# A build-time dispatcher that orders all engines of an attention and token-MLP kernel, with the softmax denominators re-laid by DMA and the MLP and output projection in one PSUM bank

## Chip, core and metric

One core of a Trainium2 chip. The metric is device time in microseconds of one execution; three executions of the kernel before took 981.83, 982.70 and 983.78, so the median is 982.7.

## What is computed

Sequence length 2048, width 512, 32 heads of 16, MLP width 1376, all inputs bf16, and `B_x` is not used:

```python
xn = _layernorm(x)                       # the same normalised x feeds both branches
# A: full attention over 2048 keys, 32 heads of 16
qkv = xn @ wqkv
p = softmax(q @ k.T * 16 ** -0.5)        # per head, 2048 x 2048
a = (p @ v) @ wo
# B: an MLP over the tokens (w1: 2048 x 1376, w2: 1376 x 2048)
h = _layernorm(xn)
u = gelu(einsum("bsd,sf->bdf", h, w1) + b1)
y = einsum("bdf,fs->bds", u, w2) + b2
out = x + a + transpose(y)
```

There are 32 heads x 2048 x 2048 = 134 million exponentials, which is where the time goes.

## The kernel before

**Blocks, key tiles and units.** The attention runs in 32 blocks, `b = 8 * qb + G`: four query blocks of 512 rows (`qb`), and eight groups of four heads (`G = 2 * T + e_`). A block walks over 16 key tiles of 128 keys. For one key tile (the code calls it a period, or group `g`) TensorE makes four score matmuls, one per head, each on its own strip of 32 rows of the array (L748, `score_group`), into two *pairs* of PSUM banks. ScalarE takes the exponential of one pair at a time, 128 x 1024 elements (L757, `exp_pair`), into one of ten buffers `pT`. Four PV matmuls then add that key tile into bank 6 (L767, `pv_group`). V carries a 17th column of ones per head, so the same matmuls sum the denominators. Banks 0 to 5 are three pairs used in turn; in block 0 only two pairs are, since banks 4 and 5 serve the first tiles' transposes and V.

**Extras.** Everything else that TensorE does goes through one more bank, number 7 (`EX_BANK`): the Q, K and V projections of later blocks (L425, L407, L569), the 11 units of the first MLP matmul (`task_ut`, 16 matmuls each, L605, then three VectorE steps, a tanh on ScalarE at L620, and one VectorE step), the 16 units of the second (`task_yt`, 11 matmuls each, L632), and the output projection of 16 row tiles (`task_outproj`, 8 matmuls each, L652). VectorE must empty bank 7 before the next extra begins.

**Order of the work.** There is no scheduler on the chip: each engine runs its own list in order and waits on semaphores. The lists are written by one loop over periods. In each period it issues the scores and exps of one key tile, the PV of the tile two periods back, and then up to `EXTRA_BUDGET = 2.0` big matmuls from a queue of extras that is sorted by hand-written due periods. Due periods put the first MLP matmul after block 4, the second one right after it, and the output projection of query block `qb` near the end of the query block after it.

**End of a block.** Bank 6 is copied to `OT32` (L688). VectorE shuffles the four denominator rows over the partitions (L695) and inverts them in four pieces of 128 columns (L700). GpSimd multiplies (L703) and leaves `oT`, which the output projection reads. The last block uses a shorter way straight from bank 6 (L712 to L719), with the last two projection matmuls per tile and the stores interleaved.

**Residual.** `task_yt` writes `0.5 * y + x` plus the bias into an f32 buffer `resid`, which takes the place of `xn` and `h`; the output projection is added to it on the way out.

**Block 0.** After four tiles are prepared, block 0 starts, and the other twelve tiles' LayerNorm, transposes, K and V of T=0 are put one tile per period behind the PV matmuls.

Of the kernel before, what the change touches and what calls it, by code (L numbers as in the profile page):

```python
# [12 lines left out]
S = 2048  # L13
# [13 lines left out]
GELU_A = 0.044715  # L27

DEBUG_SCHED = False
LAG = 2  # L30
NPB = 10
NQS = 3
EXTRA_BUDGET = 2.0
NW1 = 2
NW2 = 2

# [148 lines left out]
def bass_parallel_sum__softmax_full_mha__mixer_token_mlp__prompt_kernel(  # L185
# [18 lines left out]
    with ExitStack() as es:  # L204
# [5 lines left out]
        x_sb = sb("x_sb", [128, NT, D], BF16)  # L210
# [3 lines left out]
        resid = big.bitcast(F32)[:, :].rearrange("p (t d) -> p t d", d=D)  # L214

        def resid_alias_keys(st):
            ks = []
            for j in (2 * st, 2 * st + 1):
                ks.append(("xn", j) if j < NT else ("h", j - NT))
            return ks  # L220
# [6 lines left out]
        V17 = sb("V17", [128, NKT * H * 17 + 16], BF16)  # L227
        pT = sb("pT", [128, NPB, 1024], BF16)
        OT32 = sb("OT32", [128, 2, 512], F32)
        denb = sb("denb", [128, 2, 512], F32)  # L230
# [12 lines left out]
        u_sb = sb("u_sb", [128, 1, 512], F32)  # L243
        ga_sb = sb("ga_sb", [128, 1, 512], F32)
        osb = sb("osb", [128, 2, 512], BF16)
        ps = es.enter_context(nc.psum_tensor("ps", [128, 8 * 512], F32))

# [8 lines left out]
        def bank_bf16(i):  # L256
            return ps.bitcast(BF16)[:, i * 1024:(i + 1) * 1024] if hasattr(ps, "bitcast") else None

# [3 lines left out]
        def dma(q, dst, src, reads, writes, name="", noncontig=False):  # L262
            if noncontig:
                def fn(eng, dst=dst, src=src):
                    with nc.allow_non_contiguous_dma(reason="tiny strided vector load"):
                        return eng.dma_start(dst, src)
            else:
                def fn(eng, dst=dst, src=src):
                    return eng.dma_start(dst, src)
            return sc.add(q, fn, reads=reads, writes=writes, name=name, dma=True)  # L270
# [8 lines left out]
        v17_kh = V17[:, 0:NKT * H * 17].rearrange("p (k h c) -> p k h c", k=NKT, c=17)  # L279
        for T in range(1, 4):  # L280
            sc.add("dve", lambda e, T=T: e.memset(v17_kh[:, :, 8 * T, 0:16], 0.0),
                   writes=[("V", t, T) for t in range(NT)])
        sc.add("dve", lambda e: e.memset(V17[:, NKT * H * 17:], 0.0), writes=[("Vpad",)])
        sc.add("dve", lambda e: e.memset(v17_main[:, :, 16:17], 1.0), writes=[("Vone",)])

        sc.add("pool", lambda e: e.memset(qmask[:, 0:1], 0.0), writes=[("qmask",)])
        for r in range(4):
            sc.add("pool", lambda e, r=r: e.memset(qmask[32 * r:32 * r + 16, 0:1], 1.0),
                   reads=[("qmask",)], writes=[("qmask",)])
        sc.add("pool", lambda e: e.tensor_scalar(qmask[:, 1:2], qmask[:, 0:1], -1.0, 1.0, ALU.mult, ALU.add),  # L290
# [69 lines left out]
        def ln_tile(t, which):  # L360
            ln_stats(t, which)
            ln_norm(t, which)
# [12 lines left out]

        ps_bf = ps.bitcast(BF16)

        def kt_chunk(T, c, bk, evac_eng="dve"):
            kt_pe(T, c, bk)
            kt_evac(T, c, bk, evac_eng)  # L380

        def kt_evac(T, c, bk, evac_eng):
            evac(evac_eng, KT[:, T, 512 * c:512 * (c + 1)], bank(bk), reads=[("bank", bk)],
                 writes=[("KTt", T, t) for t in range(4 * c, 4 * c + 4)])
# [14 lines left out]
        def kt_pe(T, c, bk):  # L399
            for _ in kt_pe_gen(T, c, bk):  # L400
                pass

        def kt_pe_gen(T, c, bk):
            for ct in range(NCT):
                if ct % 2 == 0:
                    yield 2.0
                sc.add("pe", lambda e, ct=ct: e.matmul(  # L407
                    bank(bk), lhsT=wqkv_sb[:, ct, D + 128 * T: D + 128 * T + 128],
                    rhs=xnT[:, ct, 512 * c:512 * (c + 1)], start=(ct == 0), stop=(ct == NCT - 1)),
                    reads=[("wqkv", 1, T)] + [("xnT", t) for t in range(4 * c, 4 * c + 4)], writes=[("bank", bk)])  # L410

        def evac(eng, dst, src, reads, writes):
            if eng == "act":
                return sc.add("act", lambda e: e.activation(dst, src, ACTF.Identity), reads=reads, writes=writes)
            return sc.add("dve", lambda e: e.tensor_copy(dst, src), reads=reads, writes=writes)  # L415

        def qt_proj(qb, T, bk, act_first=False):
            for _ in qt_proj_gen(qb, T, bk, act_first):
                pass

        def qt_proj_gen(qb, T, bk, act_first=False):
            for ct in range(NCT):
                if ct % 2 == 0:
                    yield 2.0
                sc.add("pe", lambda e, ct=ct: e.matmul(  # L425
                    bank(bk), lhsT=wqkv_sb[:, ct, 128 * T:128 * (T + 1)], rhs=xnT[:, ct, 512 * qb:512 * (qb + 1)],
                    start=(ct == 0), stop=(ct == NCT - 1)),
                    reads=[("wqkv", 0, T)] + [("xnT", t) for t in range(4 * qb, 4 * qb + 4)], writes=[("bank", bk)])
            yield 0.0
            for e_ in range(2):  # L430
                b = 8 * qb + 2 * T + e_
                slot = b % NQS
                if act_first and e_ == 0:
                    sc.add("act", lambda e, slot=slot: e.activation(QT[:, slot, :], bank(bk), ACTF.Identity,
                                                                    scale=qmask[:, 0:1]),
                           reads=[("bank", bk), ("qmask",)], writes=[("QT", slot)])
                else:
                    sc.add("dve", lambda e, e_=e_, slot=slot: e.tensor_scalar(QT[:, slot, :], bank(bk),  # L438
                                                                            qmask[:, e_:e_ + 1], None, ALU.mult),
                           reads=[("bank", bk), ("qmask",)], writes=[("QT", slot)])  # L440

        def vT_pe(tiles, T, bk):
            for j, t in enumerate(tiles):
                for ct in range(NCT):
                    sc.add("pe", lambda e, ct=ct, j=j, t=t: e.matmul(  # L445
                        bank(bk)[:, 128 * j:128 * (j + 1)], lhsT=xnT[:, ct, 128 * t:128 * (t + 1)],
                        rhs=wqkv_sb[:, ct, 2 * D + 128 * T:2 * D + 128 * (T + 1)],
                        start=(ct == 0), stop=(ct == NCT - 1)),
                        reads=[("wqkv", 2, T), ("xnT", t)], writes=[("bank", bk)])

        def vT_evac(tiles, T, bk, evac_eng):
            n = len(tiles)
            t0_ = tiles[0]
            assert tiles == list(range(t0_, t0_ + n))
            dst = V17[:, t0_ * H * 17:(t0_ + n) * H * 17].rearrange("p (t h c) -> p t h c", t=n, c=17)[:, :, 8 * T:8 * T + 8, 0:16]
# [3 lines left out]
        NPRE = 4  # L459
        SH = 0  # L460

        def tb(t):
            return t % 2 if t < NPRE else 4

# [514 lines left out]
```

## Time and profile before

| what | value |
|---|---|
| median of three runs | 982.7 us |
| span of the profiled execution | 979.6 us |
| ScalarE (ACT) busy | 953.8 us, 97% |
| TensorE (PE) busy, clock granted between 1.0 and 0.5 | 822.8 us, 84% |
| VectorE (DVE) busy | 306.4 us, 31% |
| GpSimd (POOL) busy | 70.1 us, 7% |
| DMA | 18.34 MB, mean 19 GB/s |

The profiled execution has no device time of its own in the results; its span runs from the first to the last instruction of the program, and the median of the runs is 3.1 us longer. PEld is the load of the stationary operand, and SPq the DMA queue of SyncE. A line of the timeline is: start, duration, engine, source line, operation, output <- inputs, shape, count, and in brackets the idle time before it with what ended it; equal instructions are merged, so "x20" lasts from the first one's start to the last one's end. A line of the chain of waits is: start, duration, engine, output, source line, count. A line of the windows view is: the stretch, its length, then busy time (and count) of PE, PEld, DVE, ACT and POOL, the granted TensorE clock, the DMA share and GB/s.

### The profile page before, as it was taken

To read this page: it belongs to the slowest core of one execution; us is meant where nothing else is said; L and a number is where in the kernel's file an instruction comes from. 1 tells how busy PE (TensorE), PEld (TensorE's weight loads), DVE (VectorE), ACT (ScalarE), POOL (GpSimd) and SP (SyncE) were. 2 spreads that over 40 slices of the span, in tenths; PEclk is the share of its full clock that TensorE was granted. 3 is DMA by queue.
4 is the path that set the end of the run, shared out by engine and by line. 5 is a ranking of instruction groups with operands and counts; after the bars stand their busy time and mean duration, and the time that the engine had idled before them with its cause. 6 is when DMAs were issued, how large, how long until landed. Compare 5 with 4: busy or idle time off the path is not lost.

```text
span 979.6 us, 11965 instructions
## 1 busy us (share of the span) xinstructions
PE 822.8 (84%) x5019; PEld 208.2 (21%) x5084; DVE 306.4 (31%) x522; ACT 953.8 (97%) x1045; POOL 70.1 (7%) x110
## 2 busy tenths in 40 slices
PE   5888898787888878888888888989889898998885
PEld 3422213211111112222222222111211111111121
DVE  6666633234322343222333223122211212102233
ACT  5999999999999999999999999999999999999995
POOL 3213200000000000000000000000000000000000
PEclk9999859988878888999999999555955555555797
DMA  8000000122111100111011010000000000000000
GB/s 193 2 1 17 6 1 2 22 51 43 21 22 22 22 17 1 30 28 27 11 30 44 17 42 2 0 1 4 19 1 1 1 1 0 1 1 1 11 11 22
DMA packets 57013, 18.34 MB, mean 19 GB/s; under 512 B 50816, under 2 KB 56960, under 8 KB 56960
## 3 DMA queue, kind: packets, MB, share of 16 engines
q1 hardware_dynamic: 53792, 16.00, 7.1%
q10 hardware_dynamic: 3168, 1.57, 0.6%
q8 instruction: 40, 0.66, 0.3%
q14 instruction: 13, 0.11, 0.0%
HBM read 15.47 MB, written 2.10 MB: 18 GB/s over the span
## 4 chain that ended last, share of the span: by engine, by line
ACT 87%; PE 10%; DVE 2%; issue 1%; DMA 1%; ACTq 0%; SPq 0%; DVEq 0%
ACT pT L757 86%; PE ps L748 3%; PE ps L767 2%; PE ps L605 1%; PE ps L425 1%; DMA x_sb<-in_A_x_dram 1%; ACT ga_sb L620 1%; PE ps L389 0%; PE ps L407 0%; DVE denb L717 0%; PE ps L652 0%; DVE QT L438 0%; PE ps L445 0%; DVE osb L665 0%; DVE stats L341 0%
## 5 line engine op out<-in xcount | busy, mean ns | idle before, releaser
L757 ACT ACTIVATE pT<-ps 128x1024 bf16<-128x1024 f32 x1024 | 946.2, 1390 | 4.2 <-PE ps L748 2.6
L748 PE MATMUL ps<-QT,KT 32*128 32x512 bf16 x2048 | 448.9, 464 | 123.5 <-ACT pT L757 102.1
L767 PE MATMUL ps<-pT,V 128*32 128x512 bf16 x2048 | 240.3, 469 | 0.6 <-ACT pT L757 0.6
L748 PEld LDWEIGHTS ps<-QT,KT 32*128 32x128 bf16 x2048 | 95.3, 94 | 505.8 <-ACT pT L757 481.5
L688 DVE COPY OT<-ps 128x512 f32<-128x512 f32 x31 | 21.4, 692 | 322.0 <-PE ps L767 322.0
L700 DVE RECIPROCAL denb<-denb 128x128 f32<-128x128 f32 x124 | 108.8, 920 | 0.9
L703 POOL TENSOR_TENSOR oT<-OT,denb 128x512 bf16<-128x512 f32 x31 | 39.3, 1266 | 791.3 <-DVE denb L700 791.3
L767 PEld LDWEIGHTS ps<-pT,V 128*32 128x32 bf16 x2048 | 51.9, 97 | 148.1 <-issue 145.8
L605 PE MATMUL ps<-big,w1blk 128*128 128x512 bf16 (+1 forms) x158 | 54.5, 419 | 6.5 <-issue 3.6
L632 PE MATMUL ps<-gT,w2blk 128*128 128x512 bf16 (+1 forms) x160 | 53.0, 398 | 2.8 <-issue 1.8
L637 DVE SCALAR_TENSOR_TENSOR big<-ps,x_sb 128x512 f32<-128x512 f32 x16 | 11.1, 691 | 102.3 <-PE ps L632 102.3
L652 PE MATMUL ps<-wo_pad,oT 128*128 128x512 bf16 x107 | 35.5, 406 | 2.4 <-issue 1.7
L610 DVE TENSOR_SCALAR u_sb<-ps,b1col 128x512 f32<-128x512 f32 (+1 forms) x11 | 8.3, 751 | 74.3 <-PE ps L605 74.3
L438 DVE TENSOR_SCALAR QT<-ps,qmask 128x512 bf16<-128x512 f32 x30 | 21.1, 747 | 32.3 <-PE ps L425 32.3
L665 DVE TENSOR_TENSOR osb<-ps,big 128x512 bf16<-128x512 f32 x16 | 11.0, 688 | 52.1 <-PE ps L652 52.0
L425 PE MATMUL ps<-xnT,wqkv_sb 128*128 128x512 bf16 x49 | 21.4, 509 | 2.6 <-issue 2.6
L695 DVE STREAM_SHUFFLE denb<-OT 128x512 f32<-128x512 f32 x31 | 22.4, 721 | 0.0
L415 DVE CAST V<-ps 128x128 bf16<-128x128 f32 (+1 forms) x26 | 12.4, 477 | 22.8 <-PE ps L569 22.2
L347 POOL TENSOR_TENSOR mv<-mv,mhalf 128x1 f32<-128x1 f32 x32 | 18.2, 567 | 2.7
L407 PE MATMUL ps<-xnT,wqkv_sb 128*128 128x512 bf16 x42 | 14.7, 423 | 2.7 <-DVE KT L415 1.6
L605 PEld LDWEIGHTS ps<-big,w1blk 128*128 128x128 bf16 (+1 forms) x176 | 10.7, 101 | 28.4 <-issue 24.4
L415 DVE CAST KT<-ps 128x128 bf16<-128x128 f32 (+1 forms) x26 | 12.2, 469 | 14.4 <-PE ps L407 9.1
(59 smaller groups left out, 211.8 us busy)
## 6 DMA issues: line engine op xcount, KB each, us to landing
w1blk<-in_B_w_dram SPq DMA_DIRECT2D x10, 512.0 KB, 4.1
w2blk<-in_B_w_dram SPq DMA_DIRECT2D x16, 320.0 KB, 3.3
out_dram<-osb SPq DMA_DIRECT2D x16, 128.0 KB, 1.7
x_sb<-in_A_x_dram SPq DMA_DIRECT2D x3, 512.0 KB, 9.9
wqkv_sb<-in_A_wqkv_dram ACTq DMA_DIRECT2D x3, 384.0 KB, 11.2
wo_pad<-in_A_wo_dram SPq DMA_DIRECT2D x8, 64.0 KB, 2.0
wqkv_sb<-in_A_wqkv_dram ACTq DMA_DIRECT2D x3, 128.0 KB, 3.8
w2blk<-in_B_w_dram SPq DMA_DIRECT2D x16, 24.0 KB, 1.7
```

Of the source, the lines that this page charges most:

```text
L415: return sc.add("dve", lambda e: e.tensor_copy(dst, src), reads=reads, writes=writes)
L425: sc.add("pe", lambda e, ct=ct: e.matmul(bank(bk), lhsT=wqkv_sb[:, ct, 128 * T:128 * (T + 1)], rhs=xnT[:, ct, 512 * qb:512 * (qb + 1)], st ...
L605: sc.add("pe", lambda e, st=st: e.matmul(bank(EX_BANK)[0:m, :], lhsT=w1blk[:, slot, st, 0:m], rhs=h_sb[:, st, :], start=(st == 0), stop=(s ...
L632: sc.add("pe", lambda e, ft=ft, m=m: e.matmul(bank(EX_BANK), lhsT=w2blk[0:m, slot, ft, :], rhs=gT[0:m, ft, :], start=(ft == 0), stop=(ft = ...
L652: sc.add("pe", lambda e, G=G: e.matmul(bank(EX_BANK), lhsT=oT[:, par, G, 128 * sti:128 * (sti + 1)], rhs=wo_pad[:, G, :], start=(G == 0), ...
L688: sc.add("dve", lambda e: e.tensor_copy(OT32[:, eb, :], bank(PV_BANK)), reads=[("bank", PV_BANK)], writes=[("OT32", eb)])
L695: sc.add("dve", lambda e: e.stream_shuffle(denb[:, eb, :], OT32[:, eb, :], [16] * 32), reads=[("OT32", eb)], writes=[("denb", eb, c) for c ...
L700: sc.add("dve", lambda e, cs=cs: e.reciprocal(denb[:, eb, cs], denb[:, eb, cs]), reads=[("denb", eb, c)], writes=[("denb", eb, c)])
L703: sc.add("pool", lambda e: e.tensor_tensor(oT[:, qb % 2, G, :], OT32[:, eb, :], denb[:, eb, :], ALU.mult), reads=[("OT32", eb)] + [("denb" ...
L748: sc.add("pe", lambda e, r=r, bk=bk: e.matmul(bank(bk), lhsT=KT[32 * r:32 * r + 32, T, 128 * kt:128 * (kt + 1)], rhs=QT[32 * r:32 * r + 32 ...
L757: sc.add("act", lambda e: e.activation(pT[:, buf, :], ps[:, s_ * 1024:(s_ + 1) * 1024], ACTF.Exp, scale=0.25), reads=[("bank", 2 * s_), (" ...
L767: sc.add("pe", lambda e, r=r, buf=buf, off=off: e.matmul(bank(PV_BANK)[32 * r:32 * r + 32, :], lhsT=V17[:, off:off + 32], rhs=pT[:, buf, 5 ...
```

## The change

All the code that writes the engine lists is replaced. The instructions of a score pair, an exp, a PV round, a LayerNorm, a projection stay what they were unless listed here.

**A dispatcher at build time.** A small simulation with one table of estimated durations decides in which order instructions enter each engine's list. Every job is a generator that yields steps (engine, priority, ready test, action). Whenever an engine is free in the model, the ready step with the lowest priority value is issued and the engine is held for the estimated time:

```diff
+EST = dict(
+    start=15.5, pe_switch=0.11, mm512=0.215, mm128=0.065, pe_lat=0.25,
+    exp=0.924, exp_lat=1.45, tanh=0.75, act_lat=0.55,
...
+    pool_lat=0.1, rstd=0.95, pmul=1.3, sp=0.15, dma=2.3, dma_big=6.0,
+)
+class Dispatch:
...
+                    for ent in self.steps[e]:
+                        _, pr, ready, _ = ent[1]
+                        if not ready():
+                            continue
+                        pr = 0.9 if pr is None else pr
+                        k = (pr() if callable(pr) else pr, ent[0])
+                        if best is None or k < best[0]:
+                            best = (k, ent)
```

On PE a pair of scores has priority 0.0, a chunk of two extra matmuls 1.2 and PV a value that depends on how much is waiting; two key tiles' PV can be issued together:

```diff
+        def a_feed():
...
+                        def ready(b=b, kt=kt, T=T):
+                            return (any(is_free(("pair", i)) for i in range(3)) and done(("QT", b))
+                                    and k_ready(T, kt))
...
+                            for r in (2 * hf, 2 * hf + 1):
+                                score_mm(b, kt, r, 2 * s_ + r % 2)
...
+            if held >= NPB - 3 or len(c) >= 3:
+                return 0.8
+            if len(c) >= 2 or left_pv[b] <= 2:
+                return 1.4
+            return 5.0
...
+                per = 2 if cost is None else max(1, int(0.43 / cost))
```

Bank 7 goes to the extra with the earliest due period among those whose inputs are ready in the model, whether it is due yet or not. The queue has no budget per period any more:

```diff
+            for k, (due, rel, gen, nm) in enumerate(extras):
+                if (best is None or due < best[0]) and rel():
+                    best = (due, k)
```

**Exponentials.** The code also has a path that would make some exponentials on VectorE from bits (`d_score`, `d_bits`, `d_chain`, key tiles `D_KTS`). It is used for blocks `b >= D_FROM`, and `D_FROM = 99`, so with 32 blocks all 1024 exps stay on ScalarE. Q is scaled by `QSCALE` instead of 1 and the exp's scale divided by it. Four scalings of V into a new tile `VS` remain (`vs_scale`), and a memset of it on GpSimd in the prologue, ahead of the masks for Q.

**Denominators.** For all blocks but the last, the shuffle and the four reciprocals give way to DMAs, all on SP's queue, round one small reciprocal; GpSimd's multiply stays:

```diff
+                for r in range(4):
+                    dma("sp", rl[32 * r:32 * r + 32, eb, :],
+                        OT32[32 * r + 16:32 * r + 17, eb, :].rearrange("p (j c) -> p j c", c=16),
+                        reads=[("OT32", eb)], writes=[("rl", eb)], name="den_gather", noncontig=True)
...
+                sc.add("dve", lambda e: e.reciprocal(rl[:, eb, :], rl[:, eb, :]),
+                       reads=[("rl", eb)], writes=[("rl", eb)])
...
+                dma("sp", scr[eb].rearrange("r (j c) -> (r j) c", c=16), rl[:, eb, :],
+                    reads=[("rl", eb)], writes=[("scr", eb)], name="den_put", noncontig=True)
...
+                for r in range(4):
+                    dma("sp", denb[32 * r:32 * r + 32, :], scr[eb, r:r + 1, :].broadcast_to([32, 512]),
+                        reads=[("scr", eb)], writes=[("denb",)], name="den_spread")
```

`scr` is a small tensor in DRAM.

**Second MLP matmul and output projection in one bank.** `task_out(st)` replaces `task_yt` and `task_outproj`: 11 + 8 matmuls (11 + 6 in the last query block) add into bank 7, and one VectorE step adds bias and residual. The residual rows are read from DRAM a second time with the W2 blocks. The gelu's factor 0.5 moves into the step before it:

```diff
-                sc.add("pe", lambda e, ft=ft, m=m: e.matmul(
+                mms.append(lambda ft=ft, m=m: sc.add("pe", lambda e: e.matmul(
                     bank(EX_BANK), lhsT=w2blk[0:m, slot, ft, :], rhs=gT[0:m, ft, :],
...
+                    start=(ft == 0), stop=False),
+                    reads=[("w2blk", slot), ("gT", ft)], writes=[("bank", EX_BANK)]))
             for G in range(ng):
...
+                mms.append(lambda G=G: sc.add("pe", lambda e: e.matmul(
                     bank(EX_BANK), lhsT=oT[:, par, G, 128 * sti:128 * (sti + 1)], rhs=wo_pad[:, G, :],
...
+                    start=False, stop=(G == ng - 1)),
...
+                sc.add("dve", lambda e: e.scalar_tensor_tensor(dst, bank(EX_BANK), b2col[:, st:st + 1],
+                                                               xr[:, slot, :], ALU.add, ALU.add),
```

A tile's `task_out` may start when the first MLP matmul is complete, its W2 block is loaded, the tile before it is out, and `oT` of the query block's last group (of group 5 in the last query block) is there.

**Smaller edits.** `QT` has four slots instead of three, and one VectorE step writes both heads' versions of Q (`task_qt`). A W1 unit may start when the gelu of the one before is complete (`task_ut`). In block 0 a tile's transposes, K and V are separate jobs of the dispatcher (`tile_job`). The prologue's first four tiles and the last block's end keep their steps.

## The prediction

> **What bounds the kernel now.** First the page, for the engine that is always busy and for the clock.
>
> ```profile
> PE 822.8 (84%) x5019; PEld 208.2 (21%) x5084; DVE 306.4 (31%) x522; ACT 953.8 (97%) x1045; POOL 70.1 (7%) x110
> ACT  5999999999999999999999999999999999999995
> PEclk9999859988878888999999999555955555555797
> L757 ACT ACTIVATE pT<-ps 128x1024 bf16<-128x1024 f32 x1024 | 946.2, 1390 | 4.2 <-PE ps L748 2.6
> ```
>
> ScalarE is full from slice 2 to the last; its 1024 exps (L757) are the kernel, and they stay there. PE's 84% is not a bound, but its clock falls to half wherever only scores and PV are left (slices 29 on).
>
> ACT's share hides small losses, since an exp is issued before the one ahead has ended. So I take the pace from the longest unbroken piece of the chain of waits, 250.34 / 273 = 0.917 us.
>
> ```profile
> 394.52 250.34 ACT pT L757 x273
> 765.62 56.01 ACT pT L757 x61
> 824.40 56.01 ACT pT L757 x61
> ```
>
> By the timeline of ACT the first exp starts at 15.79 and the last ends at 968.14: 952.35 us. 1024 x 0.917 = 939.0, and 11 tanh at 0.52 (next fence) are 5.7. So **7.6 us** are lost between first and last exp, and no order of work can win more than that; the prologue (15.8) and the tail (11.5) keep their steps. Some 2 us of it lie in block 0 (ACT idles 0.98 at 22.52). The rest comes where extra matmuls meet a slow clock. The timeline round one W1 unit (first ACT, then PE):
>
> ```profile
> 204.42 0.81 ACT L620 ACTIVATE ga_sb<-ga_sb 128x512 f32<-128x512 f32 x1
> 204.94 18.96 ACT L757 ACTIVATE pT<-ps 128x1024 bf16<-128x1024 f32 x20
> 223.63 0.78 ACT L620 ACTIVATE ga_sb<-ga_sb 128x512 f32<-128x512 f32 x1
> 225.38 0.60 PE L748 MATMUL ps<-QT,KT 32*128 32x512 bf16 x2 [1.04 <-ACT pT L757]
> 225.92 0.62 PE L767 MATMUL ps<-pT,V 128*32 128x512 bf16 x4
> 226.47 1.03 PE L605 MATMUL ps<-big,w1blk 128*128 128x512 bf16 x2
> 227.44 0.61 PE L748 MATMUL ps<-QT,KT 32*128 32x512 bf16 x4
> ```
>
> A tanh costs 204.94 - 204.42 = 0.52. From tanh to tanh are 19.21 us: 20 exps and one tanh make 18.86, so 0.35 is lost per unit. On PE, start to start at half clock, a pair of scores takes 0.54 (225.38 to 225.92), a PV group 0.55, two big matmuls 0.97. The same at full clock:
>
> ```profile
> 213.88 0.39 PE L748 MATMUL ps<-QT,KT 32*128 32x512 bf16 x2 [0.26 <-ACT pT L757]
> 214.19 0.40 PE L767 MATMUL ps<-pT,V 128*32 128x512 bf16 x4
> 214.53 0.61 PE L605 MATMUL ps<-big,w1blk 128*128 128x512 bf16 x2
> 215.07 0.39 PE L748 MATMUL ps<-QT,KT 32*128 32x512 bf16 x2
> ```
>
> 0.31, 0.34, 0.54. Where the clock changes, from windows (the figure before the DMA share is the clock):
>
> ```profile
> 204.60:211.40 6.80, 5.47 (x27) 1.02 (x28) 2.39 (x4) 6.67 (x9) 1.27 (x1) 0.50 0.59 115
> 211.40:220.60 9.20, 8.02 (x57) 2.17 (x54) 0.00 (x0) 9.20 (x11) 0.00 (x0) 1.00 0.02 4
> 220.60:225.00 4.40, 2.57 (x19) 0.64 (x18) 2.69 (x4) 4.40 (x6) 0.00 (x0) 1.00 0.57 119
> 225.00:232.00 7.00, 6.28 (x31) 1.28 (x36) 3.40 (x7) 6.87 (x9) 0.00 (x0) 0.51 0.00 0
> ```
>
> The W1 burst ends at 220.6, 4.4 us without extras follow, the clock halves, and it stays half 5.4 us into the next burst (226.47 to 232).
>
> **The slack.** After the pair at 225.38 the next is due one pace later, 226.30; it comes at 227.44, 1.14 late. The one after (due 228.13) starts at 229.50, 1.37 late, and 0.35 is lost. A Q projection at half clock makes a pair 1.14 late (762.89 to 764.95 against 0.917), and there the cycle of two blocks takes 824.40 - 765.62 = 58.78, against 64 x 0.917 = 58.69: 0.1 lost. So scores may be about 1.0 us late; lateness beyond that is lost on ACT.
>
> **The change, part by part.**
>
> *The order.* Before, each key tile gets at most two big matmuls. The dispatcher gives scores priority, but whenever no pair of PSUM banks is free PE takes a chunk of two, as long as an extra holds the one extra bank: some chunk per exp. At full clock that fits (0.31 + 0.54 = 0.85 of 0.917, with PV deferred and doubled): 0 lost. Its cost table knows one clock only (0.215 per matmul, 0.11 per switch, the warm rows above). At half clock the modelled sequence pair, chunk, chunk, pair comes to 0.54 + 0.97 + 0.97 = 2.48, so the next pair is 1.56 late, and each further pair with chunk adds 1.51 - 0.92 = 0.59. Less 1.0 of slack: 0.5 for a burst of two chunks, 1.2 after the next pair.
>
> *W1 units.* A unit waits for the gelu of the one before: evacuation and two steps 0.75 + 0.69 + 0.69, tanh 0.78 with half a pace of waiting, 0.69, some 0.9 of latencies: 4.9 us, in which the clock falls as at 220.6. In the first four gaps K and V projections for T=3 run and keep it up; for six of eleven I count half clock. It reaches into the next burst for 2 to 5.4 us; the losses run from 0.4 to 1.8, I take **1.0 each, 6.0**.
>
> *MLP output and projection in one bank.* Now 19 matmuls per tile (17 in the last quarter), one evacuation instead of two, and the separate bias step goes: on VectorE about 16 x (0.69 + 0.49) = 19 us less, off the path (31% busy). But the W2 work, spread from 391 to 609 at full clock today, moves to four dense bursts after blocks 7, 15, 23 and 29, each after a stretch without extras. Same price: **4 x 1.0 = 4.0**. The last burst is 4 x 17 matmuls, some 38 us by a chunk per exp and 1.2 of evacuation, inside the 47 us or so that blocks 30 and 31 (58.7) leave after block 29's result, so it fits; if it didn't, the tail would grow by what is over, up to 10. Residual rows are read again, 16 x 128 KB beside the W2 loads: hidden, as a store of that size lands in 1.7 us.
>
> *Q projections.* Isolated at half clock: by the spans of blocks about eight (at b = 10, 14, 16, 18, 22, 24, 26, 30) instead of four. Two chunks back to back, bounds 0.1 (today's) and 0.8 (a PV behind them): **8 x 0.5 = 4.0**. One evacuation of 1024 columns for two of 0.747, between 0.75 and 1.5: hidden behind 16 periods of lead.
>
> *Block 0.* Only two bank pairs there; chunks of K, V and transposes now fall between any two scores instead of at one fixed place. Bounds 2.0 (today) and 7 (every one of 12 tiles late by 0.4): **3.5**, nearer today's since the matmuls are the same. The added memset of VS sits on POOL ahead of the LayerNorm steps: 17 times the columns of the 0.20 us one, at most 3.4, into gaps of 1.65 and 2.52; rows of x land only at 7.4: 0.
>
> *Denominators.* Out go 124 reciprocals (0.92) and 31 shuffles (0.72), 131 us of VectorE. In come 31 reciprocals of 16 columns (between 0 and 0.92) and 9 DMAs per block on SP's queue: gather, store to DRAM, spread. Each leg lands in about 1.7 to 2.0 (small loads and stores of before): copy, three legs, reciprocal, POOL's 1.27, about 8 to 9 us. Block 30's result has the whole of block 31 (29 us) as cover, block 31 keeps the old on-chip way; without cover 8 us would go on the end. What is queued behind the new waits: on VectorE the reciprocal waits for its gather, and the evacuation that frees the extra bank stands behind it, with PE's next extra and then scores behind that. Behind a 512 KB load (4.1 us) a gather is late by 2 or more; five such meetings, half of them felt. On POOL LayerNorm steps stand behind the multiply. Between 0 and 5: **1.0**.
>
> *Tanh.* The order on ACT is fixed from the model, with half a pace of margin on average; if PE ends a burst up to 1 us late, ACT waits: 0 to 5, **1.5**.
>
> Sum: 6.0 + 4.0 + 4.0 + 3.5 + 1.0 + 1.5 = 20.0 lost, against 7.6: +12.4. Span 979.6 + 12.4 = 992.0; the median of the three runs (982.7) lies 3.1 above the span, so **995.1**.
>
> The page "TensorE: Matmul & The Clock Gate" of the Trainium skill ("What's actually happening") says that one idle window of about 3.4 us halves the clock and one busy window restores it. That speaks against bursts with gaps; by its window a burst would run 3.4 us at half clock and lose about 0.9, ten of them 9 instead of 10; the rows above show up to 5.4.
>
> **Rivals.**
> 1. *Faster* (0.20): scores first keeps ACT fed, bursts warm the clock sooner and the slack takes nearly all. For it: W2 work at full clock lost nothing from 394 to 645. Block 0 at 2.0 and 1.5 for the rest: 4.1 less, 978.6. It decides where a pair at half clock stays under 1.0 late.
> 2. *Same* (0.06): the losses come to what they are today, 980.7 to 984.7.
> 3. *Denominator legs stall VectorE and PE* (0.10): gathers land 1.7 us later than planned in every block, less 1.0 of slack, 31 x 0.7 = 22 on top: 1017. Against it: all rows of small transfers.
> 4. That the change doesn't do what it says: the VectorE exponential path is never entered (D_FROM = 99); only four scalings of VS remain, under 1 us each, no price.
>
> The likeliest has 0.64, its own range 986 to 1010. With the faster rival and the edge of the third the range is **978 to 1012**. Faster by over 0.2% (2 us, what a measurement of this kernel can tell) 0.20, within 0.06, slower 0.74.
>
> **What would show it.** Right: exps at 0.917 wherever no extras run, the gaps between them longer at each W1 unit, after blocks 7, 15, 23 and 29 and at each lone Q projection, all at a clock of 0.5; L700's 124 rows gone. Wrong: W1 units at full clock throughout, losses under 8 in all, or VectorE idle in front of the small reciprocal for microseconds.

## The result, and the profile after

The changed kernel takes **1105.3 us** in the median of four runs (1092.4 to 1114.8), the kernel before 982.3 beside it: ratio **1.120**, interval 1.114 to 1.127. Executions more than 1.5% above the fastest of their kernel are left out of the ratios, and of the times given for `before_split` (there 1089.5 and 1090.9) and `legs_pace` (1119.7 and 1122.8, the one traced). The forecast was 995.1 with a range up to 1012. The profiled execution is the fastest of the four; its span is 1090.5, which is 110.9 more than before. The three others took 13 to 22 us longer, and no trace shows where.

From the page of the changed kernel, the lines that answer to those of before:

```profile
PE 984.7 (90%) x5033; PEld 221.6 (20%) x5084; DVE 165.6 (15%) x324; ACT 970.0 (89%) x1045; POOL 71.8 (7%) x111
ACT  5977967799797699999998979999999999999875
PEclk8966958578555585555555975555555985555685
L637 ACT ACTIVATE pT<-ps 128x1024 bf16<-128x1024 f32 x1024 | 960.6, 1267 | 95.8 <-PE ps L583 93.7
L767 DVE RECIPROCAL rl<-rl 128x16 f32<-128x16 f32 x31 | 7.8, 253 | 218.9 <-DMA rl<-OT 218.9
```

ScalarE's row of nines has holes in its first 14 slices (to 382 us), near 580 and 640 us and at the end, and its idle time before exps went from 4.2 to 95.8 us, nearly all of it waiting for scores (L583). PE's clock is at a half for most of the span although PE is 90% busy. VectorE, which lost half its work, sits 218.9 us in front of the small reciprocal (L767).

Counted as in the prediction (from one exp's end to the next, less 0.917, less 0.52 for each tanh between), before loses 7.5 us from the first exp's end to the last's and after 119.1; the difference, 111.6, is the whole of the 110.9. So everything is lost between exps, and the place of each loss can be read off. Block 0 to 58 us: 4.2. Six single gaps of 2.4 to 4.5 us, each behind a block's gathers: 19.7. One more of 1.65 at 88.5, behind a LayerNorm step of VectorE that took 3.61 us instead of 0.40 while GpSimd cleared `wo_pad` for 3.55. Eight lone Q projections at 0.66: 5.3. The remaining 88 come in bursts of extras, mostly in steps of 0.59 from one exp to the next.

**The single gaps.** The largest, in the chain of waits of the changed kernel (start, length, engine, output, line):

```profile
177.40 3.91 DMA rl<-OT
181.33 1.64 DMA rl<-OT
182.98 1.59 DMA rl<-OT
184.59 1.64 DMA rl<-OT
186.26 0.25 DVE rl L767
187.06 0.60 DVE KT L458
187.71 0.61 PE ps L487 x4
```

The four gathers of one block run one after the other. They fill four different strips of `rl`, but all of them are declared as writing the one key `("rl", eb)`, so the synchronisation that is laid on top of the list makes each wait until the one before it has landed; the last three take some 1.6 us each. The copy of bank 6 ended at 177.14 and the reciprocal started 9.1 us later; the dispatcher's table had planned 2.9 (four issues of 0.15 and one landing of 2.3). VectorE's list has the evacuation of bank 7 (the KT cast at 187.06) behind the reciprocal at 186.26; PE's next extra waits for bank 7, and the scores stand behind that extra in PE's order. ScalarE was idle for 4.38 us ahead of 188.90.

**The steps of 0.59.** PE's timeline of the changed kernel in the middle of a W1 unit, 267 us:

```profile
267.26 0.61 PE L583 MATMUL ps<-QT,KT 32*128 32x512 bf16 x2
267.80 1.03 PE L1004 MATMUL ps<-big,w1blk 128*128 128x512 bf16 x2
268.76 0.61 PE L583 MATMUL ps<-QT,KT 32*128 32x512 bf16 x2
```

and the windows view over that stretch (the figure ahead of the DMA share is the clock):

```profile
264.46:383.93 119.47, 114.30 (x452) 20.61 (x456) 11.65 (x18) 93.92 (x98) 3.81 (x3) 0.50 0.12 29
```

A pair of scores every 1.51 us (267.26 to 268.76) where an exp needs 0.917: 0.59 late each time, which is the step. And the clock doesn't come back: it stays at 0.50 for 119 us, with PE busy for 114 of them. It rises right after a place where two chunks fell together:

```profile
381.94 1.89 PE L1077 MATMUL ps<-wo_pad,oT 128*128 128x512 bf16 x4
383.76 0.45 PE L583 MATMUL ps<-QT,KT 32*128 32x512 bf16 x2
```

The theory to be tested (**C** in the expectations): what releases the clock is not that TensorE is busy, but how much of its array works. A matmul of 512 columns streams for 0.43 us at half clock (a chunk of two takes 0.97 start to start, of one 0.54). A lone pair of scores uses two of the four 32-row strips, half the array. Four scores in a row are two pairs beside each other: they take 0.55, no longer than one pair. So *pair, two matmuls* works (0.5 x 0.43 + 2 x 0.43) / 1.51 = 0.71 of the array, and the order of the kernel before, *four scores, PV, two matmuls* (0.55 + 0.55 + 0.97), works (0.43 + 0.43 + 0.86) / 2.07 = 0.83. These shares are worked out from the durations. The rivals: **A**, the DMA legs are the whole cause (the first expectations set **B** against it, half clock in dense bursts, which leaves open what holds the clock down), and **D**, the dispatcher's bursts are simply too dense. Any other rival is told where it stands.

### The profile page after: what moved, and what is told of

The parts are those of the page before. It is cut to its first block, busy times and chain, and to the rows that moved or that the text cites. A ratio compares the mean times of both kernels' runs of the same rounds, so it can differ in the third digit from the quotient of the medians.

```text
span 1090.5 us, 12124 instructions
## 1 busy us (share of the span) xinstructions
PE 984.7 (90%) x5033; PEld 221.6 (20%) x5084; DVE 165.6 (15%) x324; ACT 970.0 (89%) x1045; POOL 71.8 (7%) x111
## 4 chain that ended last, share of the span: by engine, by line
ACT 52%; PE 35%; DMA 7%; DVE 4%; issue 1%; POOL 1%; SPq 0%; ACTq 0%; DVEq 0%
ACT pT L637 52%; PE ps L583 13%; PE ps L666 6%; DMA rl<-OT 5%; PE ps L1072 5%; PE ps L1004 4%; PE ps L1077 2%; PE ps L487 2%; PE ps L944 1%; PE ps L926 1%; DMA xreg<-in_A_x_dram 1%; DVE big L451 1%; DMA w2blk<-in_B_w_dram 1%; DVE stats L436 1%; DVE OT L751 0%
## 5 line engine op out<-in xcount | busy, mean ns | idle before, releaser
L637 ACT ACTIVATE pT<-ps 128x1024 bf16<-128x1024 f32 x1024 | 960.6, 1267 | 95.8 <-PE ps L583 93.7
L583 PE MATMUL ps<-QT,KT 32*128 32x512 bf16 x2048 | 546.6, 545 | 48.0 <-ACT pT L637 10.0
L666 PE MATMUL ps<-pT,V 128*32 128x512 bf16 x2048 | 273.7, 549 | 5.3 <-DVE OT L751 3.0
L583 PEld LDWEIGHTS ps<-QT,KT 32*128 32x128 bf16 x2048 | 100.8, 97 | 530.9 <-ACT pT L637 389.1
L1072 PE MATMUL ps<-gT,w2blk 128*128 128x512 bf16 (+1 forms) x166 | 67.8, 498 | 10.8 <-DVE osb L1087 4.5
L1004 PE MATMUL ps<-big,w1blk 128*128 128x512 bf16 (+1 forms) x166 | 68.0, 498 | 2.6 <-issue 2.5
L934 DVE TENSOR_TENSOR QT<-ps,qmask 128x1024 bf16<-128x1024 f32 x15 | 18.3, 1222 | 176.6 <-PE ps L926 176.6
L767 DVE RECIPROCAL rl<-rl 128x16 f32<-128x16 f32 x31 | 7.8, 253 | 218.9 <-DMA rl<-OT 218.9
L487 PE MATMUL ps<-wqkv_sb,xnT 128*128 128x128 bf16 x256 | 28.1, 263 | 9.2 <-DVE KT L458 5.2
L1087 DVE SCALAR_TENSOR_TENSOR osb<-ps,b2col,big 128x512 bf16<-128x512 f32 x12 | 8.9, 740 | 123.2 <-PE ps L1077 73.6
L487 PEld LDWEIGHTS ps<-wqkv_sb,xnT 128*128 128x128 bf16 x256 | 20.0, 118 | 18.3 <-issue 7.3
L1072 PEld LDWEIGHTS ps<-gT,w2blk 128*128 128x128 bf16 (+1 forms) x176 | 12.1, 104 | 39.1 <-issue 30.5
```

The lines of the kernel that those rows point to most:

```text
L487: sc.add("pe", lambda e, ct=ct: e.matmul(bank(bk)[:, 128 * j:128 * (j + 1)], lhsT=xnT[:, ct, 128 * t:128 * (t + 1)], rhs=wqkv_sb[:, ct, 2 ...
L583: sc.add("pe", lambda e: e.matmul(bank(bk), lhsT=KT[32 * r:32 * r + 32, T, 128 * kt:128 * (kt + 1)], rhs=QT[32 * r:32 * r + 32, sl, :], st ...
L637: sc.add("act", lambda e: e.activation(pT[:, buf, :], ps[:, s_ * 1024:(s_ + 1) * 1024], ACTF.Exp, scale=EXP_SCALE), reads=[("bank", 2 * s_ ...
L666: sc.add("pe", lambda e, r=r, lhs=lhs, rhs=rhs: e.matmul(bank(PV_BANK)[32 * r:32 * r + 32, :], lhsT=lhs, rhs=rhs, start=first, stop=last, ...
L1004: mms = [lambda st=st: sc.add("pe", lambda e: e.matmul(bank(EX_BANK)[0:m, :], lhsT=w1blk[:, slot, st, 0:m], rhs=h_sb[:, st, :], start=(st ...
L1072: mms.append(lambda ft=ft, m=m: sc.add("pe", lambda e: e.matmul(bank(EX_BANK), lhsT=w2blk[0:m, slot, ft, :], rhs=gT[0:m, ft, :], start=(ft ...
```

## The experiments

All are the changed kernel with the edits named, except `before_split`, which is the kernel before. "..." in a diff stands for lines left out. The `fill` ones add matmuls whose result nothing reads.

**1. The legs apart.** Each leg gets its own key, and what reads them waits for all four; every engine's order stays the same.

```diff
-  reads=[("OT32", eb)], writes=[("rl", eb)], name="den_gather"
+  reads=[("OT32", eb)], writes=[("rl", eb, r)], name="den_gather"
...
-  reads=[("scr", eb)], writes=[("denb",)], name="den_spread"
+  reads=[("scr", eb)], writes=[("denb", r)], name="den_spread"
```

> The four gather DMAs of a block no longer wait for one another, nor do the four spreads; every engine's order of instructions is that of the changed kernel. Theory A (the serial DMA legs stall VectorE, and behind it PE and ScalarE, and that is the loss): a block's reciprocal comes about 2.5 us after the copy instead of 7 to 8, VectorE's wait for the gathers falls from 219 us to under 100, the long gaps between exps (seven of 1.6 to 4.5 us, 21 us in all) and most of what follows them go: 985 to 1010 us. Theory B (the loss is PE at half clock in the dense bursts, whatever the DMAs do): only the 21 us go, the steps of 0.59 us per exp stay: 1065 to 1085 us.

Measured: 1072.5 us, ratio 1.088 (1.081 to 1.096), in the range that B gave. SP's DMA queue at the end of the same block, in the changed kernel and then in this one:

```profile
177.40 7.69 SPq L360 DMA_DIRECT2D rl<-OT  x4
182.25 3.09 SPq L360 DMA_DIRECT2D rl<-OT  x4
```

Four gathers in 3.09 us instead of 7.69, and VectorE's wait before L767 falls from 218.9 to 115.5. That is worth some 33 us, but 91 us are still lost between exps. A is a cause, not the whole one. The 33 is rough: in this trace block 0 loses 15.3 us at half clock, where the changed kernel's trace loses 4.2 with the same code, so outside block 0 the two traces differ by 40.

**2. The legs as they are, but the table knows.** The DMAs stay serial; the dispatcher plans 8.3 us for the gathers and 8.8 for the spreads, and so puts VectorE's reciprocal where its input is nearly there.

```diff
-  at[("rl", b)] = dp.use("sp", 4 * EST["sp"]) + EST["dma"]
+  at[("rl", b)] = dp.use("sp", 7.5) + 0.8
...
-  at[("denb", b)] = dp.use("sp", 4 * EST["sp"]) + EST["dma"]
+  at[("denb", b)] = dp.use("sp", 6.5) + 2.3
```

> DMAs as in the changed kernel, but the dispatcher's table knows that a block's gather takes 8.3 us and its spread 8.8 us, so that VectorE's reciprocal is put later in its list. Theory A: as good as legs apart, since a late denominator harms nobody, only the wait in VectorE's list does: 985 to 1010 us. Theory B: 1065 to 1085 us.

Measured: 1022.9, ratio 1.041 (1.037 to 1.044); 50 us lost. Neither theory's range holds it. A right entry in the table did more here than faster DMAs under a wrong one. VectorE still waits 177.3 us before L767, so the wait as such seems to cost little, and what stands behind it to count. How much of the gain is that, and how much the different places of the chunks that the new plan brought along, this run alone doesn't tell.

**3 and 4. TensorE filled.** Where no extra holds bank 7, two useless matmuls go into it, at most once per key tile; `legs_fill` has the edit of 1 as well.

```diff
+            elif done("tiles") and fill["p"] + 1.0 <= prog["p"] < NKT * NBLK - 8:
+                free_at["ex"] = None
+                fill["p"] = prog["p"]
+                dp.spawn(task_fill())
```

> Two matmuls of no use are put into the free extra bank when no extra wants it, at most once per key tile; serial DMA legs as in the changed kernel. Theory A: PE has nothing to gain, about as before, 1090 to 1115 us. Theory B: the clock stands at 1.0 through the stretches without extras, bursts begin at full clock, and the steps of 0.59 us go but for those after a stall by the DMAs: 1000 to 1045 us.

> Both: legs apart and the filling matmuls. Theory A alone: as legs apart, 985 to 1010 us. Theory B alone: as fill, 1000 to 1045 us. If both are causes: no stall cools the clock, no burst starts at half clock, 5 to 15 us are lost between the exps, 980 to 990 us; at the low end it would be level with the kernel before.

Measured: `fill` 1035.1, ratio 1.053 (1.049 to 1.057); `legs_fill` 1007.0, a median of six that scatter from 989.6 to 1015.4, over the ranges of all three forecasts. Windows of `fill`:

```profile
220.00:820.00 600.00, 542.10 (x3393) 138.24 (x3391) 55.06 (x86) 597.74 (x656) 25.35 (x20) 0.99 0.10 25
```

614 more matmuls, and between 220 and 820 us only 2.5 us are lost, 2.2 of them in one gap at 287 behind four serial gathers, though W1 units and two bursts of `task_out` lie in there. At clock 1.0 the dispatcher's order costs nothing; most of what `fill` loses (60 us) lies between 58 and 220 us (46) and at 823 to 843 (9), in bursts that start behind late DMAs and run at half clock. It is the clock, not the amount of work: D falls in its simple form.

**5 and 6. Chunks of four.** `legs_per4` has the edit of 1, `per4` has the legs as they are.

```diff
-  per = 2 if cost is None else max(1, int(0.43 / cost))
+  per = 4 if cost is None else 2
```

> Legs apart, and an extra goes to PE in chunks of four matmuls instead of two (K, V of single tiles: two groups instead of one); everything else is planned by the same rules. Theory C (the clock rises only when enough of the array works in a window: a lone pair of scores fills half of it, so pair and two big matmuls at half clock come to (0.5 x 0.43 + 0.85) / 1.51 = 0.71 and the clock stays down however busy PE is; pair and four come to (0.5 x 0.43 + 1.71) / 2.45 = 0.79 and it rises): bursts are at half clock for one or two windows only, the rows of 0.59 us steps break off: 990 to 1020 us. Theory D (bursts are just too dense for the half clock, and longer chunks make scores later still): 1060 to 1100 us, as legs apart or worse.

> The changed kernel with its four-leg DMAs as they are, and chunks of four matmuls instead of two. Theory C: what the bursts lose goes (some 70 of 112 us), what the DMA legs cost stays: by addition legs_per4 1007 plus the 33 us by which the changed kernel lies above legs_apart, 1040 us, range 1025 to 1055. If the legs cost mostly because a stall halves the clock and the clock then stays there, chunks of four take a part of that too: 1015 to 1030. Rival (DMA legs alone): above 1080.

Measured: `legs_per4` 1006.9, ratio 1.025 (1.018 to 1.031); `per4` 1042.8, ratio 1.062 (1.057 to 1.067). There is twice the extra work between two pairs, and yet a burst of `legs_per4` loses 0.6 to 2 us where it had lost 0.59 per exp. At half clock *pair, four matmuls* takes 0.54 + 1.82 (the row at 381.94 above) and works 0.82 of the array. The two causes nearly add up: without legs and with chunks of four 98.4 us are gained, and the single edits gain 32.8 and 62.5.

**7. The same amount, at most once per key tile.**

```diff
-  yield ("pe", 1.2, lambda: True, go)
+      paced["p"] = prog["p"]
+  yield ("pe", 1.2, lambda: prog["p"] >= paced["p"] + 1.0, go)
```

with chunks of three and the edit of 1.

> Legs apart, and at most one chunk of three matmuls per key tile, so that two pairs of scores stand for one chunk. C and D both: at half clock two pairs, PV and chunk need 0.54 + 0.55 + 1.40 = 2.5 us per key tile against 1.83, and use 0.86 of the array, so the clock rises after a window or two and a burst loses 0.5 to 1.5 us: 988 to 1005 us. If the clock has nothing to do with it and the stalls of VectorE for the denominators do the rest: 1050 to 1080 us.

Measured: 1072.9 and 1076.8, ratio 1.094 (1.090 to 1.098). A miss: no better than `legs_apart`. The order that came out is *pair, three matmuls, pair, PV*: the pairs stay alone, and 0.71 of the array is at work. That fits C, but I saw it only afterwards.

**8 and 9. Both cures with fill.**

> Legs apart, chunks of four, and the filling matmuls (two per key tile while the extra bank is free). Theory C: the clock stays at 1.0 nearly throughout and comes back by itself after a fall, so the scatter of legs with fill (990 to 1015 us) goes: 978 to 990 us. Theory D: as legs with fill, 990 to 1015 us, or worse.

> Legs apart, one chunk of three per key tile, and the filling matmuls. C and D: clock at 1.0 after block 0, 3 to 8 us lost between the exps, the last projections reach some 3 us past the last exp: 975 to 988 us, on either side of the kernel before.

Measured: `legs_per4_fill` 998.3, ratio 1.012 (1.007 to 1.016), two levels (985 to 986 and 997 to 1001); `legs_pace_fill` 1001.6, ratio 1.017 (1.013 to 1.022). Both miss what C gave, and the first lies in D's range. What the trace of `legs_per4_fill`, from the upper level, still loses is 15 us in block 0, at half clock, and 9 us between 89 and 110, where SP's queue shows the cause:

```profile
88.27 14.59 SPq L361 DMA_DIRECT2D wo_pad<-in_A_wo_dram  x8
```

Eight loads of `wo_pad` that, again, write one key and run one after the other, with a block's gathers behind them at 102.90.

**10. The test on the kernel before.** No DMA touched, nothing of the change in it: of the two extra matmuls of a key tile one moves between the two pairs of scores. A small edit that keeps the budget right is not shown.

```diff
-                score_group(period)
+                score_group(period, (0, 1))
+                if bank_q and bank_q[0].req == 1.0:
+                    bank_q[0].advance()
+                    used = 1.0
+                score_group(period, (2, 3))
...
-            budget = EXTRA_BUDGET if period < END else 1e9
+            budget = EXTRA_BUDGET - used if period < END else 1e9
```

> The kernel before, nothing of the change in it, except that of the two extra matmuls of a key tile the first stands between the two pairs of scores (pair, one matmul, pair, PV, one matmul) instead of both behind all four scores and PV. Same matmuls, same number per key tile, no DMA touched. Theory C (the clock comes back from a half only when enough of the array works in a window; a lone pair of scores fills half of the array): four scores, PV and two matmuls at half clock fill (0.43 + 0.43 + 0.85) of 2.0 us, 0.85, and recover; split they fill (0.43 + 0.43 + 0.85) of some 2.6 us, 0.66, and stay at half clock once an idle stretch has brought them there. A key tile then takes 2.6 us against 1.83; with a third to all of some 210 key tiles with extra matmuls stuck, 1030 to 1140 us. Rival (the place of the extra matmuls does not matter; the bursts of the changed kernel are slow for their DMAs or their density): 980 to 990 us.

Measured: 1067.3 and 1067.5, against 983.1, **84 us slower** (1.086), in the range that C gave. Its clock, and PE's timeline:

```profile
PEclk8999679855555757566997696755555555555587
```

```profile
211.54 0.61 PE L605 MATMUL ps<-big,w1blk 128*128 128x512 bf16 x1
212.08 0.61 PE L748 MATMUL ps<-QT,KT 32*128 32x512 bf16 x2
212.62 0.61 PE L605 MATMUL ps<-big,w1blk 128*128 128x512 bf16 x1
213.16 0.61 PE L748 MATMUL ps<-QT,KT 32*128 32x512 bf16 x2
213.70 0.62 PE L767 MATMUL ps<-pT,V 128*32 128x512 bf16 x4
```

A key tile takes 2.71 us (211.54 to 214.25) instead of 1.83, with 0.63 of the array at work, and the clock stays at a half. It is the same kind of loss as in the changed kernel, made from the old one by the place of one matmul.

**11 and 12. Scores in fours.** `quad` is after with the edit of 1, the loads of `wo_pad` apart too, the table corrected (gather 2.4 + 1.6, spread 1.8 + 2.0), and chunks of three only behind the second pair; `quad_fill` adds the fill.

```diff
+  yield ("pe", 1.2, lambda: prog["p"] >= paced["p"] + 1.0 and prog["p"] % 1.0 == 0.0, go)
```

> The changed kernel with the gathers, the spreads and the loads of wo_pad each under a key of its own and the table corrected for them, and with an extra chunk (three matmuls, at most one per key tile) allowed only behind the second pair of a key tile, so that late scores go out four at a time. Theory C: four scores, PV and three matmuls at half clock fill 0.86 of their time, so each burst recovers within some 3 to 6 us and loses 1 to 2 us; with 25 bursts and block 0 cold or not, 980 to 1000 us. Rival (a dispatcher that fills TensorE is slow whatever the order; pace as in legs_pace): 1050 to 1100 us, as legs_pace measured 1098.

> quad with two useless matmuls into the free bank per key tile, so that TensorE has hardly an idle window. Theory C: the clock hardly falls, so 976 to 990 us, below legs_per4_fill (998) and, if block 0 stays warm, at or below the kernel before. Rival (what is left in legs_per4_fill is DMA stall, not clock): no better than 998.

Measured: **1201.4** (ratio 1.221, 1.215 to 1.227) and 1399.6 (1.425, 1.419 to 1.431). Far off. PE's timeline of `quad` shows why:

```profile
416.69 0.62 PE L666 MATMUL ps<-pT,V 128*32 128x512 bf16 x4
417.24 0.61 PE L583 MATMUL ps<-QT,KT 32*128 32x512 bf16 x2
417.77 1.46 PE L1075 MATMUL ps<-gT,w2blk 128*128 128x512 bf16 x3
419.17 0.61 PE L583 MATMUL ps<-QT,KT 32*128 32x512 bf16 x2
```

The chunks obey the gate, but PV steps between the pairs (another PV group starts at 419.70): *pair, PV, pair, three matmuls*, 0.71 of the array again, and the clock is at 0.5 from 53 us to the end but for two short stretches. The fill adds work to a TensorE that is the bound.

**13. The same with PV behind the second pair too.** One edit to `quad`:

```diff
-  return pv_state["b"] < NBLK and is_free("pv") and bool(pv_cands())
+  return pv_state["b"] < NBLK and is_free("pv") and prog["p"] % 1.0 == 0.0 and bool(pv_cands())
```

> quad missed because the PV rounds, not gated, stepped between the two pairs of a key tile: its order on TensorE is pair, PV, pair, three matmuls, which fills (0.21 + 0.43 + 0.21 + 1.28) of 3.03 us, 0.70 of the array, as legs_pace did. This kernel is quad with one edit: PV too is allowed only behind the second pair, so that the order is four scores, PV, three matmuls; same matmuls, same DMAs, same pace. Theory C (the share of the array decides): at half clock it fills 0.85, as the kernel before does, and recovers; 980 to 1000 us. Rival (a chunk of three at the end of every key tile, or a dispatcher's density, holds the clock at a half whatever the order): 1150 to 1210, as quad measured 1201.

Measured: **989.2**, ratio 1.006 (1.002 to 1.009): 212 us less than `quad` with the same matmuls, DMAs and pace. The median lies between two levels of five runs each, 982.2 to 984.3 and 994.1 to 995.6. PE's timeline at the start of a burst:

```profile
293.93 0.62 PE L666 MATMUL ps<-pT,V 128*32 128x512 bf16 x4
294.48 1.46 PE L1075 MATMUL ps<-gT,w2blk 128*128 128x512 bf16 x3
295.87 0.61 PE L583 MATMUL ps<-QT,KT 32*128 32x512 bf16 x4
296.42 1.46 PE L1075 MATMUL ps<-gT,w2blk 128*128 128x512 bf16 x3
299.64 0.39 PE L583 MATMUL ps<-QT,KT 32*128 32x512 bf16 x4
```

Now late scores go out four together in the time of two, and from 299.46 on the clock is at 1.0, 6.8 us after it fell. A burst costs some 0.54 us.

The orders beside each other, at half clock, all with TensorE busy throughout:

| order | us | something streams | of the array | clock |
|---|---|---|---|---|
| before_split | 2.71 | 0.79 | 0.63 | stays |
| after: pair, 2 | 1.51 | 0.85 | 0.71 | stays |
| quad, legs_pace: pair, 3, pair and a PV | 3.02 | 0.85 | 0.71 | stays |
| per4: pair, 4 | 2.36 | 0.91 | 0.82 | rises |
| before: 4 scores, PV, 2 | 2.07 | 0.83 | 0.83 | rises |
| quad2: 4 scores, PV, 3 | 2.49 | 0.86 | 0.86 | rises |

The share of time in which anything streams does not order them (0.85 stays, 0.83 rises); the share of the array does, with a border between 0.71 and 0.82. That is a fit to six orders. Shown is the order's effect itself, both ways, by `before_split` and `quad2`.

The traces can be asked more closely. In all 18 the granted clock changes only in steps of 3.41 us. For each such window the array's share follows from the matmuls in it: 0.43 us at half clock, 0.21 at full clock, for 512 columns, times the part of the array that the matmul covers. Of 117 windows at half clock with a share of 0.755 or more, 113 are followed by full clock; of 2502 below it, 48 are, and in 26 of these a weight load stands without its matmul, whose record is missing, so the share is read too low.

The border of 0.755 is the best fit and puts 52 of the 2619 windows on the wrong side; the best border in the share of time in which anything streams puts 134 there, where calling none a rise puts 161. The fall goes by the share too: at full clock 177 of 198 windows under 0.365 are followed by half clock, and 2 of 2631 above it, though TensorE was busy for half the window or more in most of those that fell. So scores and PV alone, (0.21 + 0.21) / 1.83 = 0.23 of the array at full clock, let the clock fall, and the two matmuls of a fill raise it to (0.21 + 0.21 + 0.43) / 1.83 = 0.46.

**14 to 16. What is left.** `quad2_fill` (which also lifts the gate on chunks once all scores are out), `lwt_per4_fill` (legs and loads apart, table corrected, chunks of four, fill), and `quad3_fill`, which is `quad2_fill` with block 0's transposes and K and V projections, too, only behind the second pair:

```diff
-  yield ("pe", 1.0, lambda: done(("xn", t)) and is_free("b4"), tp)
+  yield ("pe", 1.0, lambda: done(("xn", t)) and is_free("b4") and prog["p"] % 1.0 == 0.0, tp)
...
```

> quad2 with two useless matmuls into the free bank in key tiles that have no chunk, so that TensorE has hardly an idle window. Theory C: the clock hardly falls behind block 0: 975 to 988 us. Rival as for quad2: 1300 to 1400 us, as quad_fill measured 1400.

> legs_per4_fill (998) with the eight loads of wo_pad under keys of their own and the table corrected for gather and spread. Its profile lost 9 us between 89 and 110 us behind those loads and 15 us in block 0 at half clock. If those were the causes, 9 us go and the block 0 part may or may not: 976 to 991 us. Rival (the loss at 89 us is the place of the gather in SP's order, not the loads waiting for one another): 995 to 1000 us.

> quad2_fill measured 975.5 to 977.1 us in five runs and 985 to 990 in seven. Its block 0 still has transposes and K and V projections between the two pairs of a key tile, an order that at half clock fills (0.21 + 0.43 + 0.43 + 0.21 + 0.85) of 3.1 us, 0.69. This kernel is quad2_fill with those, too, allowed only behind the second pair (0.84). Theory C: block 0 leaves half clock in every run, and all runs lie at 974 to 980 us, below the kernel before. Rival (the two levels of quad2_fill come from elsewhere): two levels again, median 984 to 988.

Measured: `quad2_fill` 986.2, ratio 0.999 (0.995 to 1.002), in two levels, 975.5 to 977.1 and 985.4 to 990.4; `lwt_per4_fill` 992.9, ratio 1.005 (1.001 to 1.008), also in two levels, 979.5 to 982.3 and 992.5 to 994.2, with 3.5 left of the 9 us at 89 to 110; `quad3_fill` **976.6**, ratio **0.994** (0.993 to 0.995), all six runs between 973.9 and 978.2. So the upper level is most likely block 0 at half clock: the upper-level traces of `legs_per4_fill` and `lwt_per4_fill` lose 15.1 and 15.3 us there, `quad2_fill`'s lower-level trace 4.2, and its upper level has no trace. With it gone this version is faster than both kernels. From its page:

```profile
ACT  5999999999999999999999999999999999999995
PEclk8999998999989999999999999999999999999998
```

2.7 us are lost between exps, against 7.5 in the kernel before and 119.1 in the changed one.

## Why the prediction was wrong, point by point

- *Pace, what can be won, where the loss lies.* Right: 0.917 us is the median from exp to exp in every kernel here but the two that TensorE binds (`quad` 0.918, `quad_fill` 1.087), all 111 us lie between exps, and the best version wins some 6 us of the 7.6 that the prediction gave as the limit.
- *Slack of 1.0 us and the step.* Right in size: "each further pair with chunk adds 1.51 - 0.92 = 0.59" is to the digit what the bursts lose. The prediction had the price and not the count.
- *The failed step:* "It reaches into the next burst for 2 to 5.4 us", and with it the 1.0 per W1 unit and 1.0 per dense burst, 10.0 together. The time to recover was read from bursts of the old order, four scores at a time, and carried to a new order with lone pairs. There a burst doesn't recover before chance puts two chunks together: up to 119 us at a half. Some 88 us stand where 10 were put; part of them hangs on the DMA legs, whose stalls set off bursts at half clock. The rows of before held no lone-pair burst at all, so this cost should have had an open upper bound: every exp of every burst, 0.59 each.
- *The skill's rule.* The page "TensorE: Matmul & The Clock Gate" of the Trainium skill ("What's actually happening") has one busy window restore the clock. No window of the stretch from 264 to 384 us did, with TensorE busy for 114.3 of 119.5 us. The measurement decides: busy is not enough, and by the windows above the share of the array at work separates the cases.
- *Denominators, 1.0 (0 to 5).* Wrong. "Three legs, 8 to 9 us" took the four gathers of a block, and the four spreads, as parallel; they share a key and run in a row. The chain that the prediction named (reciprocal, evacuation behind it, PE's extra, scores) is the one that the trace shows; six gaps make 19.7 us, and by `legs_apart` the whole effect, half clock after the stalls included, is some 33. Its sign of being wrong, "VectorE idle in front of the small reciprocal for microseconds", is L767's 218.9 us.
- *Rival 3* had this mechanism at 22 us, with a chance of 0.10. Its direct price was near, but it was the smaller cause, and 1017 is far from 1105.
- *Block 0, 3.5:* 4.2 in the changed kernel's trace, but that is luck: with the same code in block 0 the trace of `fill` loses 2.8 and those of `legs_apart` and `plan_serial` 15.3, above the 7 that the prediction gave as the upper bound. *Q projections, eight at 0.5:* eight at 0.66. Right.
- *Rival 4:* the VectorE path is never entered, as said.
- *The bank shared by MLP and output projection* cost nothing by itself: in `fill` its two bursts at full clock lose nothing.

## What to carry to other kernels

A build-time order with one duration per instruction has no way to see that the order sets the clock: give it matmuls that fill the array in one piece (all row strips together, other work behind them), and test an order at half clock, where the backlog decides whether it drains. When DMAs write separate pieces of one tile, give each piece a key of its own, or this kernel's synchronisation runs them in a row, and write into the table what the trace measures. A recovery time belongs to the order it was measured in.

## What was not expected of the hardware

TensorE at half clock stays there for as long as its work fills too little of the array, with a border near 0.75 in windows of 3.41 us: 119 us at a stretch in the changed kernel, over 850 us in `quad`, with TensorE busy nearly throughout. Four scores on four row strips take 0.55 us at half clock, two take 0.54, so where scores are late, issuing them together doubles their rate. And some 500 to 600 useless matmuls made the kernel faster where TensorE would otherwise have idled and the order could drain (1105.3 to 1035.1 for `fill`), and slower where it couldn't (1201.4 to 1399.6 for `quad_fill`).
